# Two attention blocks on one core: octets of batches worked in turn by pairs, with K loaded for two octets at once

## The chip, the core and the metric

The kernel runs on one core of a Trainium2 chip. The core has a matrix engine (TensorE, PE in the profile), a vector engine (DVE), a scalar engine (ACT), a general engine (GpSimd, POOL) and a queue engine (SyncE, SP), which here issues all transfers between HBM and on-chip memory. PE writes its results to eight banks of accumulation memory (PSUM); DVE and ACT read them there. The metric is the device time of one execution in microseconds (us); lower is better.

## The reference

Two independent problems, A and B, of the same shape are computed and their outputs set side by side. One of them, cut to what matters:

```python
B, Sq, D = 16, 80, 576
Hq, Hkv, Sk, Dh = 32, 16, 512, 128           # two query heads share one K/V head
q = (x @ wq).reshape(B, Sq, Hq, Dh).transpose(0, 2, 1, 3)
k, v = repeat(k_cache, 2, axis=1), repeat(v_cache, 2, axis=1)
scores = einsum("bhqd,bhkd->bhqk", q, k) * Dh ** -0.5
o = einsum("bhqk,bhkd->bhqd", softmax(scores), v)
out = o.transpose(0, 2, 1, 3).reshape(B, Sq, Hq * Dh) @ wo
```

All tensors are bfloat16. K and V are 33.5 MB each for one problem, 134 MB together for both.

## The kernel before

**Units and octets.** The work is cut into 128 units. A unit is one batch row with four K/V heads, which is eight query heads. Eight units with the same four K/V heads and the batches of one half (0 to 7 or 8 to 15) form an octet; there are 16 octets. `unit(g)` (L372) orders them: problem, pair of head groups, half, head group within the pair. So octets 2i and 2i+1 have the same batches and neighbouring head groups; their K heads lie next to each other in HBM.

**Steps of a unit.** The 640 query rows of a unit (8 heads of 80) are held as five blocks of 128 rows, four from one K/V head each and a fifth with the 32 rows left over from each. K comes through a transposing transfer (`em_ldk`, L628, 512 KB) into one of NK = 7 slots of `kT`; V comes plainly (`em_ldv`, L632, 512 KB) into one of NV = 5 slots of `v_sb`. PE multiplies queries and K (L675 for whole blocks, L662 for the left-over block, two units at a time); DVE takes the row maximum (L684); ACT takes the exponential with a row sum (L688); DVE inverts the sums (L694); POOL scales the block (L697). PE transposes the five blocks (40 matmuls, L729), DVE or ACT moves the result to `pT` (L740 to L749), PE multiplies with V (16 matmuls, L772) and DVE or ACT moves that to `oT` (L786).

**Projections.** Queries for two batches and four query heads are one session of 16 matmuls (L544) and a tail of 4 (L559), moved to `qT` by ACT or DVE (L572, L573). Sessions run one per unit, about 11 units ahead of use (LQ = 11). The weights of one head group (`wq_sb`, 1 MB and two small `wt` pieces) have two slots and serve both halves. The output projection of a pair of head groups is 40 groups of 8 matmuls (L821, two per 128-row block and column half), whose results are kept (L832) or added and stored (L849, L855). Its weights come in four transfers (L600).

**What sets the order.** Every operation is put in a list with a stream name and a key (`S.add`). `arrange` (L176) then places all operations by the string ORDER: each letter takes the next operation of one stream, an apostrophe moves an operation from DVE to ACT (or to the other engine of its pair), and a digit names the PSUM bank. Each engine, SP among them, runs its operations in exactly that order, and `finalize` (L198) derives the waits. SP is one queue: while its next transfer waits for a slot, all transfers behind it wait too.

**Order of the units.** `steps` (L477) runs the first 12 octets one after another, all eight units of an octet before the next. The last four octets (two pairs, units 96 to 127) already go in turn: one unit of the first octet, one of the second, and so on. `sess` (L480) orders the query sessions to match.

Of the kernel before, what the change touches and what calls it, by code (L numbers as in the profile page):

```python
# [13 lines left out]
LA = 11.5  # L14
NK = 7
NV = 5
# [3 lines left out]
NS = 32  # L20
VK = 8.0
# [30 lines left out]
WQ1 = -16.8  # L52
# [8 lines left out]
nEJni7HHHHJHMak3j4LEMk4j5j7LKj5Hd3Jd6IdIj2'ABj1ad0Le6e5od3Llodd2'AK'Bd6lf0adpe4'Ad3omd5EBle2CdLuf0'Boe7'Ad4uoG  # L61
le1j3aole6d5CLle2uodd3'Bvple1d5NoumdAe7'Ad6old3BlCodug0245'Buld1xz'ye2Jk3d7Khwe5oadd3Alod4'ACBf06ludpd7upe1me2
d5o'Be0'Aoj4ldoc3'AcaCd1mCBuj7sle5vLd6Lludog2347'Bue0'wc6'xoulchd3tNhle2vCAd5a'youg16'zve0y'wd4u'Axld7o'Bf13zl
dpe2'Bc6pk5me0cCc7o'Aucmd1Ctuaj4loc7ucK'se3Ld2'suole7vg45olCe0u'zxe6hwd3C'Boauld5oue2'yAdlc7uoe1e4'Avoj0'BclLd
3olf05Ctuc6lpchd7ulsae1pmg26ome4ye0'w'xoc5'Ae2lod3'zod1lBe6cClouhg47atlvCe0ye5'w'xc2locd4'Bslc6CAvf12o'ze3ucpl
e0c7uCpcmc5uatc'sod1'tume7oug56loud2C'xz'yud3'wBlhue6e1holug05alw'ACCof67u'A'ye4pve2lovmoc1uc'xlCc6pue0c'zsd4u
loc5ute1mhcBe2uad6log37o'slCe0uwd5'xzluc1Coc'Be2u'ye7Ae6'td3ovlog14ulhoFd0lyFc2'xcF'zCBe1ud7lFswuc3ao'Ace2v'tf
56olg34Cplue1z'xumd2oc4cwlCe5Auo'yd0upc3ld1vB'scg57e4'yo'td5'ze3'wd7lAxe2o'Bb4Coluhbluhamg23Cue0b6ouqlbCuc4vqc
e0'sc6uocc4'yzc'te2h'sd3olac4xclwg06A'B'tf12w'ye5p'zd4xb6mpome0e1aob'Aloe2lCc7Bue5oclb3usloe0e1hCCc7loubaovlcq
ule2d5ou'tf06qlug17pme2zb3'wo'yae0'Ac7olce1bC'spulxoue2mc7e0ovd4lhCocvI'qe6d1lthuCBg37hluoaf25'ywuze0'x'Ab3upl  # L70
o'Bd4Cple1ud6Comuc7ce0luCc2cmubtoug25'qsulac7vye1e3oe0vb2oloblCule1qd3ho'zcad2xlCwe0vsc5'Aocug17'tC'Buf45'yzuc
6lpcuc7wcmpe0b1at'A'xo'se7md3o'Be6c4lblCve0h'qcc7Gusd5houchog24'tIulaf17y'w'zd6AlCe2e4uob3'xuBlpe0d5oc2coblsmp
g24lqe1wmc3Cocvd0'Aylue7d6xo'te1'ze2CBe3lb4oColavg57olue1wbzu'Ayuc7'qcole0ue2e5ohld4uhxd3ClBauc1o'scuog06lte7l
wc2Cocuc1'x'sAe5uc'zBd2lof46t'yd3Clpug17pmuhc5a'ywve0xe4CmAcud1o'Bue2slc3ocve6'zd5olg07Ctloe4d3'xz'yhe2'BChoc0
vlcIc7wouclac5e6tulcof47u'sAe2lc0pud1'spmcg56Comutd4luxe0d7'zo'yg26walCBue5A'xc1'yCue0woe3'zcvc2o'sd6luBcoc1'A
ue7hlcoac4d5lte0'scolg23Ctluf17wz'xue4'Ab0'yp'Bome2c3aoe6ld5Coue1lcpd4ule2obvmolg67h'qhle1xGb0wo'zI'yCae2Aud7'
BCole6ue5Coc4lcve1tbluovsc4lcCoc3u'scqe2lud4ouf06tlg15upue2'wb3'zAmb'yCovhe0e1aluob7ould5xp'Bd2lqc4e0mcog13'sC
Clve6e4'zobau'wouc3'qxcylue0d7Bluc1oc'Ad6'the2'sf45alg13pob0'zx'wCmBue3pbluCoc4ue2yld6vhoe1'Acaumqd3oc7lcg05ls
Cu'tf27z'ye1'xpd4Cb5omvpluae0bomuwe1Bu'Ac2ole7cc3o'qe6le0tchd5olag12lb7'sxo'Bze6lbCoue0lqd3uwc7o'ye2he6'ACocvl
ad5oulg14Cu'tf02wlzud7'Apu'xc4e6'Bpcme5b3oolhe0bCaolv'suc6qle5d4yumcg13tof02'ywxc6'zAe1'Bcohc7le4acColue3b5o't  # L80
ulsc7e1plcd4omc6Ccsvd3tupg07aCuCe6y'xb'wulzu'Bd0Come1ve7qld3oue2a'Ac5oulg46oulcCyb1v'wlxCuA'zf47Bushc6e0phue2c
hoe5mubJoluod3ltd4'qCpe0ulg26oud5'yze1mxe2wc6olcc7Acloe0c3'scold1Be6lCg24oua'tC'suCf07xlyue3'zpe2c6v'Boe4md1uo
'wclud0AJolvhg35thlupJe2c6'yxad4wmze3o'Be5c'Aoe0lc7cColuc2Cd1'svC'toclue7g36olud5uyle0Fsv'zd3xhwe2'BuoFc7'Ak6F
ouclg14FCKluhe0a'tuCe2'woc7'Avcz'yf56ulxd1ou'sc4plce0td7mpe2'Bog45mCoulc3cxe6zulc0co'Bd5'wyld7te2'sd4og36Ale0'
ze1ob2'wCylubCoue0aluc3ocb6'AuxlsvCBc5crue0e1obvohlue2hrd3lDCoe0uag67'toluf15x'zwd2'ype7lBd6omc3cAc0lsce1'tg34
ople0b7hwzDe1oac4bylCCc'xumre0d3ou'Bc7'Asd5ulocve2Clc4Coe1ue6a'tcolb0vo'sulg27uf14y'zub'wp'xuaAme2pc7clBd3rmd5
oe0g16lohle4Dzb2h'wx'yCDCoud6'tIBe0ulaf17ov'Ae5pblupme4Cd3ovmc1cule0sc7ucog15'turloe7b2a'x'yolze1e4lboole0e7rc
5'wCcB'Auhd2lohc3uohcle1Id4slCDog06uD'tCuaf57z'x'wud3Bpb6uCpmue4bo'AumCyvc5ld2vclc7ug01ruscc4'tze6ae5'x'wb7ool
e1bo'ylCBe0vcole2he6ud5oDlud1arlog07Alc2Csucc3'wz'tuf46xe2pb7Bmpbaome1rc'ye4Coe6lvc7d0o'Aucloe2ud5ClGtusDg17lo
huhe4'yzc3aclCe1oue7b6olvsc2uxf34o'Blcbtlpd5mrd7wAg26pCe0'xuc3'yBe1cmoud7'wc2lAcd4o'zaCg05sluCte6u'ywc3oe1'Avc  # L90
'xe0ole2uc7olhd6zhle1BacCd5ov't'soluf07e4lupg23oumpc1'x'ycBd0lwze2c5'scCmoe4uc3e1Ah'tue7lCacod5u'sColg26uoluc3
zcle4uwe1od6'Av'xd7y'Ble0og25h'tolDc4cI'ye3sc1ald2Cwvo'xe4'ze0Aucld5ou'tCof36luc1plcuc4Bc'sCe0amCug17o'tvple3b
# [174 lines left out]
def bass_concat_heads__gqa_block_cached__gqa_block_cached__near_ridge_kernel(  # L267
# [27 lines left out]
    with ExitStack() as es:  # L295
# [32 lines left out]
        def R(res, ver):  # L328
            return (res, ver)
# [151 lines left out]
        for g_ in range(NG - 2 * NPP):  # L481
            for m_ in range(8):
                sess[g_, m_] = g_ * 8 - LQ + m_
# [450 lines left out]
```

## Time and profile before

| | us |
|---|---|
| median of 3 runs | 745.14 |
| lowest and highest of them | 742.85, 745.35 |
| the profiled execution | 743.02 |
| its span, first to last instruction | 741.1 |

The profile page gives, for that execution, the busy time of each engine and groups of instructions by source line with their count and mean duration. Matmuls are pipelined: the mean of one (233 ns for a matmul of 160 columns) is its whole passage, and the next one starts well before it ends. The chain of waits lists instead what each step added to the chain that ended last, which for a row of matmuls is their pace. A view by windows gives busy time, granted PE clock (1.00 in the whole run) and transfer rate in stretches of the span.

### The profile page before, as it was taken

The page shows a single profiled execution, that of the slowest core. Times are in us where ns is not written, and L with a number is a line of the kernel's source. Part 1 is how long each engine was busy: PE and PEld are TensorE (multiplying, and loading weights), DVE is VectorE, ACT ScalarE, POOL GpSimd, SP SyncE. Part 2 cuts the span into 40 slices and gives each one's busy share as a digit, 9 for nine tenths or more (in the row PEclk, how much of TensorE's full clock was granted, in tenths as well). Part 3 has the DMA queues.
Part 4 walks back from the last instruction along what each step waited for, and adds up shares of the span by engine and source line. Part 5 has one row for each costly group of instructions (what it writes and reads, how often), then busy time and mean ns, then how long its engine had stood idle before and what let it go on. Part 6 is the DMA issues. An engine that isn't in the chain of part 4 may idle for free.

```text
span 741.1 us, 28948 instructions
## 1 busy us (share of the span) xinstructions
PE 728.4 (98%) x12103; PEld 565.7 (76%) x12103; DVE 643.0 (87%) x1469; ACT 640.6 (86%) x1835; POOL 433.8 (59%) x650
## 2 busy tenths in 40 slices
PE   7999999999999999999999999999999999999998
PEld 5777677787777777777787767777878777778777
DVE  2999788899789989899888998889988798899994
ACT  2999788899888988789878998799988898899994
POOL 0557537566556745646665564565754664657783
PEclk9999999999999999999999999999999999999999
DMA  8999999989998959999968999999999799999970
GB/s 222 225 225 237 262 234 256 227 172 264 217 201 210 265 127 209 243 263 219 232 142 202 234 298 216 224 257 240 209 215 224 155 227 236 201 216 207 238 211 22
DMA packets 364402, 160.91 MB, mean 217 GB/s; under 512 B 276464, under 2 KB 360688, under 8 KB 364272
## 3 DMA queue, kind: packets, MB, share of 16 engines
q1 hardware_dynamic: 364272, 159.05, 99.2%
q8 instruction: 96, 1.57, 0.9%
q14 instruction: 34, 0.28, 0.1%
HBM read 87.65 MB, written 2.95 MB: 122 GB/s over the span
## 4 chain that ended last, share of the span: by engine, by line
PE 84%; ACT 11%; DVE 3%; DMA 1%; issue 0%; SPq 0%; POOL 0%
PE ps L821 19%; PE ps L544 18%; PE ps L772 16%; PE ps L675 13%; PE ps L729 9%; ACT p_sb L688 7%; PE ps L559 4%; PE ps L662 4%; ACT pT L740 2%; DVE negmax L684 2%; ACT oT L786 1%; DMA acc<-in_A_x_dram 1%; ACT qT L572 1%; DVE pT L742 1%; DVE qT L573 0%
## 5 line engine op out<-in xcount | busy, mean ns | idle before, releaser
L697 POOL TENSOR_SCALAR p_sb<-p_sb,rinv 128x512 bf16<-128x512 bf16 x640 | 432.0, 695 | 289.4 <-DVE rinv L694 288.9
L688 ACT ACTIVATE p_sb<-ps,negmax 128x512 bf16<-128x512 f32 x640 | 444.2, 712 | 48.0 <-DVE negmax L684 43.8
L684 DVE TENSOR_REDUCE negmax<-ps 128x1 f32<-128x512 f32 x640 | 420.5, 682 | 36.5 <-PE ps L675 24.9
L772 PE MATMUL ps<-pT,v_sb 128*128 128x160 bf16 x2048 | 193.1, 233 | 1.6 <-issue 0.8
L544 PE MATMUL ps<-xT,wq_sb 128*128 128x160 bf16 x2048 | 180.4, 234 | 1.3 <-ACT pT L740 0.4
L821 PE MATMUL ps<-wo_sb,oT 128*128 128x288 bf16 x1280 | 180.9, 286 | 0.0
L675 PE MATMUL ps<-kT,qT 128*128 128x512 bf16 x512 | 179.6, 381 | 0.6 <-ACT p_sb L688 0.2
L772 PEld LDWEIGHTS ps<-pT,v_sb 128*128 128x128 bf16 x2048 | 152.5, 98 | 33.8 <-ACT p_sb L688 3.0
L544 PEld LDWEIGHTS ps<-xT,wq_sb 128*128 128x128 bf16 x2048 | 149.0, 98 | 26.4 <-ACT pT L740 2.0
L821 PEld LDWEIGHTS ps<-wo_sb,oT 128*128 128x128 bf16 x1280 | 122.0, 98 | 41.5 <-ACT oT L786 1.1
L688 ACT ACTIVATION_READ_ACCUMULATOR p_sb<-ps,negmax 128x1 f32 x640 | 144.1, 225 | 0.0
L740 ACT COPY pT<-ps 128x512 f32<-128x512 f32 x152 | 89.7, 607 | 11.2 <-PE ps L729 10.5
L729 PE MATMUL ps<-ident,p_sb 64*128 64x64 bf16 x5120 | 96.1, 190 | 0.3
L729 PEld LDWEIGHTS ps<-ident,p_sb 64*128 64x128 bf16 x5120 | 88.2, 95 | 2.8 <-issue 0.8
L742 DVE COPY pT<-ps 128x1024 bf16<-128x1024 bf16 x104 | 70.6, 684 | 12.5 <-PE ps L729 10.0
L572 ACT ACTIVATE qT<-ps 128x320 bf16<-128x320 f32 x135 | 59.5, 455 | 12.9 <-PE ps L559 11.5
L786 DVE CAST oT<-ps 128x320 bf16<-128x320 f32 x123 | 58.9, 481 | 9.2 <-PE ps L772 8.7
L675 PEld LDWEIGHTS ps<-kT,qT 128*128 128x128 bf16 x512 | 48.3, 97 | 22.2 <-ACT p_sb L688 3.9
L786 ACT CAST oT<-ps 128x320 bf16<-128x320 f32 x133 | 57.7, 445 | 8.4 <-PE ps L772 7.7
L573 DVE TENSOR_SCALAR qT<-ps 128x320 bf16<-128x320 f32 x121 | 57.7, 481 | 6.7 <-PE ps L559 3.6
L749 DVE COPY pT<-ps 128x256 bf16<-128x256 bf16 x138 | 37.7, 283 | 10.6 <-PE ps L729 9.4
L694 DVE RECIPROCAL rinv<-rowsum 128x3 f32<-128x3 f32 (+1 forms) x256 | 38.5, 160 | 4.0 <-ACT p_sb L688 3.8
(33 smaller groups left out, 199.1 us busy)
## 6 DMA issues: line engine op xcount, KB each, us to landing
v_sb<-in_A_v_cache_dram SPq DMA_DIRECT2D x64, 512.0 KB, 4.9
v_sb<-in_B_v_cache_dram SPq DMA_DIRECT2D x64, 512.0 KB, 4.9
wo_sb<-in_A_wo_dram SPq DMA_DIRECT2D x8, 576.0 KB, 7.5
wo_sb<-in_B_wo_dram SPq DMA_DIRECT2D x8, 576.0 KB, 6.8
wq_sb<-in_B_wq_dram SPq DMA_DIRECT2D x4, 1024.0 KB, 7.0
wq_sb<-in_A_wq_dram SPq DMA_DIRECT2D x3, 1024.0 KB, 8.3
out_dram<-osb SPq DMA_DIRECT2D x40, 72.0 KB, 4.0
wq_sb<-in_A_wq_dram SPq DMA_DIRECT2D x4, 256.0 KB, 3.2
```

The source lines that it names most:

```text
L544: last = e.matmul(ps[:, vbq[h].phys, QO + 160 * r:QO + 160 * r + 160], lhsT=wq_sb[:, wsl, ck, hi * 128:(hi + 1) * 128], rhs=xT[:, half, ck ...
L572: return e.activation(dst, src, AF.Identity, scale=SCALE)
L675: return e.matmul(ps[:, vb.phys, :], lhsT=qT[:, qsl, bl, gl * 160:gl * 160 + 128], rhs=kT[:, ks, :, gl * 128:(gl + 1) * 128], start=True, ...
L684: return e.tensor_reduce(negmax[:, si:si + 1], ps[:, vb.phys, :], axis=AX.X, op=AluOpType.max, negate=True)
L688: return e.activation(p_sb[:, psl, :], ps[:, vb.phys, :], AF.Exp, bias=negmax[:, si:si + 1], scale=1.0, accum_out=rowsum[:, ss, k:k + 1])
L697: return e.tensor_scalar(p_sb[:, psl, :], p_sb[:, psl, :], rinv[:, ss, k:k + 1], 1.0, op0=AluOpType.mult, op1=AluOpType.mult)
L729: last = e.matmul(dst, lhsT=p_sb[64 * h:64 * h + 64, psls[k_], j * 128:(j + 1) * 128], rhs=ident[64 * h:64 * h + 64, 64 * h:64 * h + 64], ...
L740: return e.copy(pT[:, pts, :, :].bitcast(F32)[:, :, 32 * h:32 * h + 32], ps[:, vtp[h].phys, :].rearrange("p (n c) -> p n c", n=16))
L742: return e.tensor_copy(pT[:, pts, :, 64 * h:64 * h + 64], psb[:, vtp[h].phys, :].rearrange("p (n c) -> p n c", n=16))
L772: last = e.matmul(ps[:, vo.phys, off:off + 160], lhsT=v_sb[:, vs, gl, j * 128:(j + 1) * 128], rhs=pT[:, pts, 4 * gl + j, :], start=(j == 0 ...
L786: return (e.copy if en == "act" else e.tensor_copy)(dst, src)
L821: last = e.matmul(ps[:, vb.phys, 0:DC], lhsT=oT[:, hi, rb * 128:(rb + 1) * 128], rhs=wo_sb[:, wi, c3 * DC:(c3 + 1) * DC], start=(hi == 0), ...
```

## The change

All 16 octets go in turn by pairs (ILV = 0), not the last four alone. One transposing transfer of 1 MB brings the K heads of both octets of a pair for one batch, so there are 64 K transfers for 128 units. `kT` holds three such buffers (NK = 6 units, where there were 7), and V has six slots (NV = 6, where there were 5). A unit reads its K half from the shared buffer through `k_of`: rows of 128 keys lie 1,024 elements apart there, where they lay 512 apart. A buffer is refilled when both units have read it. The weights of the second head group are loaded earlier (WQ1), since the second octet now starts with the first. ORDER is written anew, as are the engines and the banks that it names.

```diff
-NK = 7
-NV = 5
+NK = 6
+NV = 6
+ILV = 0
-WQ1 = -16.8
+WQ1 = -21
 ORDER = """
...
-        kT = sb("kT", [128, NK, 4, 512], BF16)
+        kT = sb("kT", [128, NK // 2, 4096], BF16)
...
-        steps = [(g_, b_) for g_ in range(NG - 2 * NPP) for b_ in range(8)]
-        for g_ in range(NG - 2 * NPP, NG, 2):
+        steps = [(g_, b_) for g_ in range(ILV) for b_ in range(8)]
+        for g_ in range(ILV, NG, 2):
             steps += [(g_ + i_ % 2, i_ // 2) for i_ in range(16)]
...
+        def k_of(U, g4):
+            pr_, r_ = divmod(U % NK, 2)
+            if steps[U][0] >= ILV:
+                return kT[:, pr_, :].rearrange("p (j n) -> p j n", j=4)[:, :, r_ * 512 + g4 * 128:r_ * 512 + g4 * 128 + 128]
+            return kT[:, pr_, r_ * 2048:(r_ + 1) * 2048].rearrange("p (j n) -> p j n", j=4)[:, :, g4 * 128:(g4 + 1) * 128]
...
-            def em_ldk(e, kc_ap=kc_ap, b=b, q=q, ks=ks):
-                src = kc_ap[b, 4 * q:4 * q + 4, :, :].rearrange("g (p j) d -> (g p) j d", j=4)
-                return e.dma_start_transpose(kT[:, ks, :, :], src)
+            def em_ldk(e, kc_ap=kc_ap, b=b, q=q, ks=ks, w=2 if goct >= ILV else 1):
+                src = kc_ap[b, 4 * q:4 * q + 4 * w, :, :].rearrange("g (p j) d -> (g p) j d", j=4)
+                dst = kT[:, ks // 2, ks % 2 * 2048:(ks % 2 + w) * 2048].rearrange("p (j n) -> p j n", j=4)
+                return e.dma_start_transpose(dst, src)
...
-            S.add("sp", 5.0 * gfirst[U] + 0.5 * (U - gfirst[U]) - LA - KK, em_ldk, writes=[R(("kT", ks), U)],
-                  dsem="d_k%d" % ks, name="ldk%d" % U, stream="K")
+            if goct < ILV or U % 2 == 0:
+                S.add("sp", 5.0 * gfirst[U] + 0.5 * (U - gfirst[U]) - LA - KK, em_ldk,
+                      writes=[R(("kT", (U + i_) % NK), U + i_) for i_ in range(2 if goct >= ILV else 1)],
+                      dsem="d_k%d" % ks, name="ldk%d" % U, stream="K")
...
-                                                    rhs=kT[:, ks_, :, g4 * 128:(g4 + 1) * 128],
+                                                    rhs=k_of(U_, g4),
...
-                                        rhs=kT[:, ks, :, gl * 128:(gl + 1) * 128], start=True, stop=True)
+                                        rhs=k_of(U, gl), start=True, stop=True)
```

The order in which SP issues its first transfers, before (left) and after (right), by the names of the code; a number is the unit, the octet or the half:

```
x half 0, first part               x half 0, first part
wq octet 0, piece 0, two wt        wq octet 1 (1 MB)
wq octet 0, piece 1                x half 0, second part
x half 0, second part              wt octet 1, wq octet 0 piece 0, wt octet 1, two wt octet 0
wq octet 0, piece 2                wq octet 0, pieces 1 to 3
K 0                                K 0 and 1 (1 MB)
wq octet 0, piece 3                x half 1, first part
x half 1, first part, two wt       K 2 and 3
K 1, K 2                           x half 1, second part
wq octet 1 (1 MB)                  V 0, V 1
K 3, x half 1 second part          K 4 and 5
V 0, K 4, K 5                      V 2, K 6 and 7
V 1, V 2, K 6, K 7                 V 3, two wo, K 8 and 9
```

More of the change, by code (lines that the diff above doesn't have):

```diff
@@ L66 @@
[L66 to L80, printed above, removed]
@@ L126 @@
[L126 to L128 removed]
+nEJni7GJIHIHMHj3k4Hj5LLHEHad3j7Md5j6k2LKdd4A'Bj6d3Ldj5A'Bd6d3dd4Bd1dd3A'B'AJKd0LaEdd4'A'Bd5e0e1odf2'Aod3lpe7d4
+lodme0Ad6'Boe1ld3BJloe2hdhCe7old4uaoe0lvd5Cole1NudAf2ld7up'Be6ouj0md3Llodf02'ABd1'Bp'Ak3j4lpd5CmLdue7Be6md4ou'
+Ae0CCd5loudKvlhAg1237oaN'Be4u'wj6x'zk5oe1ule2j7LuK'yolg0356LlCof47u'xz'yc1uclpj3vd5CLme2upc6e3'w'suoe4cmd1holF
@@ new lines @@
+g07CouFltc2av'ycxe6B'wd3u'zse0loc7d2olce1ltg46o'Ae0le7od5'zc1Colucc6scluxd0Ct'wv'yf17A'Budpe6'Be2ud3Cpme0uoc4m
+cud1A'sholg57FCoFlue4zad6'yvolf27uwc5lpcd0A'x'tpe4mg35o'Bd2C'zyve1lwc5uocme3c4suc'Aoe5ld7te6loe4b1xo'Ble3Cobul
+oub5lqhCluhe0e1hoe6ug34aolbCo'xu'yClue0qd3w'Bvd5'zAoulf17g24ulppmc6cc0scc1'tzc'xe6'sd0Cwumoc4e1u'ycod7'Avltc2e
+3Bclhog46hCsalue1wc5o'xe2u'ycd3z'Bv'Ae4tle7d6Coub5oluoe0lbolc4'qcf12'slg57pCe4uy'xb0'wmBhuC'zhod5uhc7Alcavpe1e
+6boutle4Coe3ud7mquc1olcg02vo'slCc6uyce1x'te4uzd0'wlod6'Be2olb3olc7Cue1lbou'Ach'qf25shlg34apCpc7u'zcb1C'wC'yuA'
@@ new lines @@
+xmve0e4od3muc2t'Bucold5vslf67ug02pub'wz'xmpc4'Be2q'ye6oe5h'Acd1holhd3Colug02lud6y'tv'we5'zxc4Bcmc2oe0e3'sCcoau
+c7'tcAle4ue2oc1lcsd5olg07tob3'x'zy'wlBe1e0oblCoulc7he2e5uhocc4v'se1qclCd7uth'Ad3Coluf06olug24Cplub5'zumve1e4'x
+oab'yu'wCpluc2comud0sc1'qe6le2ocd5'Atlg47o'BCf16uw'ze3lpub7'yCAvmoe2e0ve4ob'xluoc1uC'qcle3usd7aolc1ucp'Bd2log0
+5tld4z'xe1'wB'yd3Cmoe0uc5oclug26slAIf15C'zxGue7'ye0hob6v'BIoluhe2Ce3plbuo'wumd7CAv'qe0oc4lcuoc6lcutc2clpe1e4oa
+d3's'tog06ld2'wz'yd1xmBc6e0lAe3cCoue7'sg45Colvoc6'zuce0'ytd5uloe6ub4hlCoIule3e7uob'xa'wlvBCd0'AqulCf16ovg24plu
@@ new lines @@
+c3'yzuce7mwd2xuCo'sc4'Bce1'td3olg04AhlGe7'yc5Ccx'zvpb1wumoe0e4uobluole6uc7o'qcld0tc1A'Bf47'slcpe2'sd3Comug56pl
+ue1xc4'zwaco'ye2d6t'Aloc5cc4lsce0Bd5mCove1g23tluof47u'zwAe0lb3pI'xo'Bhe1mbhCou'yhpe6hluc4oe2cld5Covle0d1saulqg
+46ouCe2'wxub3'yBmuoe1lc4oblzclc7e0d6'qo'Ace1'sc3oe2lcd5t'tlog07f34w'zxe1'Ab7'yolCCe0ublouplc6ve1cmoad2uCd0Clqu
+sc3'Bcug67'tuf15'zxupe3'yb7u'w'BAmvoc6ce0C'sd4uhole2hvbolhuhpld3qg06Cpuc7'wzu'xd2'yAc'Be0mhe6oc3c'td4ole1sc7lC
+coug03htluCe6yd7'wv'x'zAe1d0umoc3uocle2Bc5'scole6hg34Ctlauof15'wvC'Axb2zlup'Bue7e6'yobumolc3qce0ld4oe1e2Csld6v
@@ new lines @@
+og37upub0xmBole6e5abzlo'wc7'yCcqu'Ae1oc3le0ud4old6ole2c'tc5sclCg17ou'thf03v'ywhAe5'xu'ze1ob4lCo'Bc7lcCpvd6se2m
+uc5ocld7uhte0lug15oauCle2wbuo'zuyle0d5Ad1xCC'Boue2'qg67pulob4u'w'yzlue0bomCAle2uFc7ocFve6'sd3oFluf07FCqlve5pc4
+'xcupd6'tmBc2cog14'slc2ye0'x'zcwe5oe1'Ad4moc3clCBd7vtlc6ouJe0e2'scoulg35tulof16'wC'zyd0u'ACe5xlue3Bc4cpud7h'sC
+oe2umJb4Joulaoe1ulbolpg35lre2w'ze4Cyc1u'xb5ovAbluComue0rcld3uoe2'Bvd5loag46le0z'tc7'xe2'ywcoc6'se1k4olcd7o'Ac0
+lBcCd3Kluf25'tvhCsg14DupDc6wuhcz'Ad0mupd4'xCymug27Buf15t'x'Bc3p'ye6caoc4mcsd2'twle1e4b3'zCo'Aue7oe0lvboluod6lr
@@ new lines @@
+g14lphe7z'yc3Dc'wohme0c4hb1olCAlue5xcoe2u'te7ad0'sCBule4obuolvc3Colce2urc6lcoue1e7sd5log34'tColuf26C'zvb1'x'wu
+'yAe4lpue0d3oDubholvc7'Brcle4d5oamg01slb7y'z'wp'Ae0c4Come1ucbltuoe2d3loe0d4rDlohe1'xg67hCBluhof25'wDu'zAc0'yCc
+pue7'sc3Cd6lxvoc'Buc0mthcd4Cuplg13u'suc7z'x'we0'ycvoe2'Be3ac1'Auoe4lcoc6lctd0Cmse7vd2olug15Ctluf36z'w'xu'yb4o'
+AuBle0e1hod5hc7plce2Csbmvouod7lurg03lpDe1'ze4oc2'yce3x'thb0o'walAe2Blc5obolcCre1luc7oe4d3uold2Csclue0Cg15'toum
+uf47'w'yb6vpGxumCDe1pbhvlAIoue4'zId3Blue0Cod5uCrg12luoDb6'xau'Blue5bmo'ze0c7'yod4lre1colc2e6cCslud5Co'tg07u'wl
@@ L129 @@
+e2suc7locDug0136ho'tluhf47xyDlc1e5we3p'zcc2o'se0e6mcoc1hlcCtc4ucolvt'splug2345ome1b0Cwluoe2'zyue7e6lbo'xolg134
+5rloDc2e0'yxacCwe7lvof34'zCuCc1ob6lvplue0pcme5Cubomuoe7lc3tue4rclc1usDco'shug0256'tolue1b3zlo'we7'ye0xCboluolu
+e2rg1456lCoDuf37'xh'zCwc0uCp'ye1cule6oe5b4vmpovlc2csublouClg0136rvDe4'ywc5uthc'zoe0uc3'scxmCug1256tlouc7c'ywe3
+zuc4'xlcsg1256o'tc7C'xy'zcue0'sc4wovclc7tculc6sb5Cubucg2347tb0y'z'x'wc7cc3scbtrb7DrDbb5brDrD
 """
@@ L475, in bass_concat_heads__gqa_block_cached__gqa_block_cached__near_ridge_kernel @@
                   name="xte%d" % half, stream="xe2")
-        steps = [(g_, b_) for g_ in range(NG - 2 * NPP) for b_ in range(8)]
-        for g_ in range(NG - 2 * NPP, NG, 2):
+        steps = [(g_, b_) for g_ in range(ILV) for b_ in range(8)]
+        for g_ in range(ILV, NG, 2):
             steps += [(g_ + i_ % 2, i_ // 2) for i_ in range(16)]
         sess = {}
-        for g_ in range(NG - 2 * NPP):
+        for g_ in range(ILV):
             for m_ in range(8):
                 sess[g_, m_] = g_ * 8 - LQ + m_
-        for g_ in range(NG - 2 * NPP, NG, 2):
+        for g_ in range(ILV, NG, 2):
             for i_ in range(16):
@@ L659, in em_qkr @@
                             last = None
-                            for _, vb_, ks_, qsl_, bl_, _ in group:
+                            for U_, vb_, ks_, qsl_, bl_, _ in group:
                                 for g4 in range(4):
```

90 lines of the change are left out of this document (36 added, 54 removed).

## The prediction

> **What bounds the kernel now.** I read the page's busy times first, then the chain of waits, PE's groups by line in two stretches of the span, and last the transfers. The page says that PE is nearly always occupied, with DVE and ACT not far behind:
>
> ```profile
> PE 728.4 (98%) x12103; PEld 565.7 (76%) x12103; DVE 643.0 (87%) x1469; ACT 640.6 (86%) x1835; POOL 433.8 (59%) x650
> DMA packets 364402, 160.91 MB, mean 217 GB/s; under 512 B 276464, under 2 KB 360688, under 8 KB 364272
> q1 hardware_dynamic: 364272, 159.05, 99.2%
> ```
>
> PE's 98% hides gaps, because a matmul's record spans its whole passage. The chain of waits shows the pace of each kind of matmul where nothing holds it up (start, us, what):
>
> ```profile
> 29.85 0.55 PE ps L662 x8
> 31.30 0.43 PE ps L675 x2
> 297.93 0.24 PE ps L559 x4
> 479.99 0.98 PE ps L821 x8
> 481.40 1.11 PE ps L544 x16
> 482.75 0.58 PE ps L729 x40
> 489.79 0.55 PE ps L772 x8
> ```
>
> So a matmul of L544 or L772 costs 0.069 us, L821 0.1225, L675 0.215, L662 0.069, L559 0.06, L729 0.0145. A unit has 16 of L544, 16 of L772, 10 of L821, 4 of L675, 4 each of L662 and L559 and 40 of L729: 1.11 + 1.11 + 1.225 + 0.86 + 0.275 + 0.24 + 0.58 = 5.40 us. 128 units are 691 us of PE work, which the change leaves as it is. The span is 741.1 us, so about 50 us are start, tail and gaps; only these can be won.
>
> Where the gaps are is seen by counting PE's work in two stretches. The first runs from the first transposition of unit 8 to that of unit 96 (72.3 to 572.1 us; 3520 transpositions are 88 units, or 11 octets), where octets go one after another:
>
> ```profile
> L772 PE MATMUL ps<-pT,v_sb 128*128 128x160 bf16 x1416 | 134.9, 233 | 0.8 <-issue 0.8
> L821 PE MATMUL ps<-wo_sb,oT 128*128 128x288 bf16 x896 | 126.9, 286 | 0.0
> L544 PE MATMUL ps<-xT,wq_sb 128*128 128x160 bf16 x1408 | 123.7, 233 | 1.1 <-ACT pT L740 0.4 <-DVE qT L573 0.3 <-issue 0.3
> L675 PE MATMUL ps<-kT,qT 128*128 128x512 bf16 x351 | 123.4, 381 | 0.6 <-ACT p_sb L688 0.2
> L729 PE MATMUL ps<-ident,p_sb 64*128 64x64 bf16 x3520 | 66.1, 190 | 0.1
> L559 PE MATMUL ps<-xT,wt 64*128 64x160 bf16 x356 | 27.8, 234 | 1.0 <-ACT qT L572 0.4 <-ACT oT L786 0.2 <-POOL p_sb L697 0.2
> L662 PE MATMUL ps<-kT,qT 128*32 128x512 bf16 x352 | 27.1, 384 | 0.6 <-ACT p_sb L688 0.3 <-ACT oT L786 0.2
> ```
>
> By the prices above this is 98.3 + 109.8 + 97.7 + 75.5 + 51.0 + 21.4 + 24.3 = 478 us of work (0.5 more for ten small transposes) in 499.8 us: 21.3 us of gaps, 1.94 us per octet. The second stretch, 572.1 to 664.7 us, holds units 96 to 111, which the kernel before already works in turn:
>
> ```profile
> L821 PE MATMUL ps<-wo_sb,oT 128*128 128x288 bf16 x192 | 27.5, 286 | 0.0
> L772 PE MATMUL ps<-pT,v_sb 128*128 128x160 bf16 x256 | 24.3, 233 | 0.0
> L675 PE MATMUL ps<-kT,qT 128*128 128x512 bf16 x64 | 22.4, 380 | 0.0
> L544 PE MATMUL ps<-xT,wq_sb 128*128 128x160 bf16 x256 | 22.3, 233 | 0.0
> L729 PE MATMUL ps<-ident,p_sb 64*128 64x64 bf16 x640 | 11.9, 190 | 0.0
> L662 PE MATMUL ps<-kT,qT 128*32 128x512 bf16 x72 | 5.5, 384 | 0.0
> L559 PE MATMUL ps<-xT,wt 64*128 64x160 bf16 x68 | 5.3, 234 | 0.0
> ```
>
> That is 23.5 + 17.8 + 13.8 + 17.8 + 9.3 + 5.0 + 4.1 = 91.2 us of work in 92.6: 0.7 us of gaps per octet. So the trace of before holds a sample of the changed order, and its PE is fuller. The longest waits of ACT and DVE, and two stretches of equal length (length, then busy PE, weight loads, DVE, ACT, POOL, then clock, DMA share, GB/s), say what the gaps hang on:
>
> ```profile
> ACT p_sb L688 <- DVE negmax L684: 43.8, 73, 1.8
> DVE negmax L684 <- PE ps L675: 24.9, 52, 2.0
> 253.00:344.10 91.10, 90.08 (x1512) 69.86 (x1510) 83.36 (x188) 77.38 (x223) 52.78 (x79) 1.00 0.97 210
> 572.10:664.70 92.60, 92.60 (x1548) 73.39 (x1546) 80.76 (x181) 81.10 (x234) 54.88 (x82) 1.00 1.01 212
> ```
>
> Score blocks queue at DVE (ACT waits for the maximum 73 times), a PSUM bank comes free late, and PE misses it. DVE is 91.5% busy in the first of these stretches and 87.2% in the other, while ACT goes the other way. No row shows PE waiting for a K or V transfer after the start.
>
> **The change, part by part.**
>
> *In turn, and the new order.* Eleven octets, those from unit 8 to unit 95, change from one kind of order to the other. If each comes down from 1.94 to 0.7 us of gaps, 13.4 us go; if the new order is no smoother than the old, nothing. Below nothing is excluded only by DVE's and ACT's unchanged number of maxima and exponentials (640 each), so I let a loss of 2 us stand. The built order speaks for the gain: priced by the mean durations of their groups, DVE's and ACT's work exceeds PE's within stretches of two units by 15 us in all, where it did by 27. I take 1.13 us, two thirds of the way, since the sample is 16 units alone: 11 x 0.81 = 8.9 us won. What is late next is DVE again.
>
> *K in 64 transfers of 1 MB, three buffers.* The bytes are the same, and the pieces too: K comes in rows of 256 B before and after. SP's own time:
>
> ```profile
> 4.95 3.61 SPq L630 DMA_TRANSPOSE kT<-in_A_k_cache_dram  x1
> 302.43 6.13 SPq L630 DMA_TRANSPOSE kT<-in_A_k_cache_dram  x2
> SPq L630 <- PE ps L772: 39.9, 12, 4.0
> DMA to landing us min/median/max: 4.3/6.5/12.5
> ```
>
> Two K issues in a row hold SP for 6.13 us, 3.1 each, so one of 1 MB should hold it about 6 us, and V, wq and stores behind it wait that long. V has six slots now; in the built order there are 26 us of PE work (median) between the moment SP can reach a V transfer and its use. For K that window shrinks. A buffer is free when both units have read it; from there (or from what SP must wait for ahead of it) to the first matmul that needs the new K lie 15.6 us of PE work in the median, where it was 23.5, or 16.7 us of time at 741/691. A 1 MB transfer needs about 6.1 + (6.5 - 3.1) = 9.5 us from issue to landing. The narrowest window, 9.8 us of work or 10.5 us, just holds it; five of 61 are under 12.4 us. The ends: 0 us lost if 9.5 holds; if landing takes the longest seen plus the second half, 12.5 + 3.1 = 15.6 us, 19 windows are too short by 34 us in all, of which I count half, since a stall also lengthens the next window: 17 us. The price is nearest to the row of two back-to-back issues; I take 0.5 us for a queue that is now and then fuller.
>
> The Trainium skill says in "DMA: Bandwidth & Descriptors", section "Rules for kernel authors", that most bandwidth needs 128 partitions and at least 1 MiB per DMA. The rows above do not bear on 1 MB transposes; since pieces stay at 256 B, I give the rule no part in the sum. By the figure of 261 GB/s for transposes in its section "Latency and other measured facts", 1.05 MB would take an estimated 4.0 us to move, and the 0.5 us would be 0.
>
> *The start.* The second octet now starts with the first, and SP brings its weights first.
>
> ```profile
> L675 PE MATMUL ps<-kT,qT x512: 379/379/391, 14.6 to 726.3; 128*128 128x512 bf16 x171
> 0.00:20.00 20.00, 15.76 (x128) 10.27 (x128) 6.28 (x18) 5.78 (x14) 1.69 (x9) 1.00 0.90 230
> 20.00:50.00 30.00, 29.91 (x499) 23.16 (x496) 27.51 (x64) 27.69 (x80) 19.09 (x30) 1.00 1.13 214
> 50.00:100.00 50.00, 47.41 (x860) 35.55 (x858) 41.69 (x96) 44.55 (x130) 28.40 (x42) 1.00 1.13 248
> ```
>
> Ahead of the end of the first K there are 4.14 MB in SP's queue (2.18 before); at 230 GB/s that is 18.0 us, so the first score matmul starts at 18 to 19 us, not 14.6. PE is not idle for it: 12 half sessions and 5 tails stand ahead of that matmul, where 3 and 1 did, which is 9 x 0.55 + 4 x 0.24 = 5.9 us of work pulled forward. PE would gain about 2 us here. Next, K for units 8 and 9 stands after 12.35 MB: 20 x 0.230 + 30 x 0.214 = 11.0 MB at 50 us, and 1.33 / 0.248 = 5.4 us more, 55.4 us. The PE work ahead of its first use is about 43 us, so PE cannot be less than 12 us behind its work there, about where the kernel before is. DVE and ACT get their first block 3.4 us later, and this may carry through the first 60 us. Ends: 2 us won, 3.4 us lost, and I take 1 us lost.
>
> *The tail.* Between the transposition of unit 112 and that of unit 120 the new order gives DVE 87 operations, where it was 82, 39 of them maxima (37 before) and 7 wide copies (3):
>
> ```profile
> L684 DVE TENSOR_REDUCE negmax<-ps 128x1 f32<-128x512 f32 x640 | 420.5, 682 | 36.5 <-PE ps L675 24.9
> ```
>
> At 0.68 us for a maximum, and about the same for a wide copy, less three projections and moves, that is 2.9 us more DVE work in a stretch that has little PE work to hide it. Ends 0 and 2.9; I take 1.5.
>
> *Sum.* -8.9 + 0.5 + 1.0 + 1.5 = -5.9 us against the profiled execution's 743.0 us: **737 us**. That execution lies 2.1 us under the median of 745.1, as the lowest run does; from the median it would be 739. I keep 737.
>
> **The rivals.**
>
> *R1, the gaps stay.* The smaller gaps of the last octets would come from what stands in them and not from working in turn. For it: a single stretch of 16 units is the evidence. Against it: DVE's share in the table. Then 743.0 + 0.5 + 1.0 + 1.5 = 746 us.
>
> *R2, slower: K comes too late.* Three buffers give a window of 16.7 us in the median, and a 1 MB transfer behind V transfers may take 15.6 us. It decides from about 12.4 us on; at 15.6 it costs 17 us, 737 + 17 = 754 us. For it: landings of up to 12.5 us for half the bytes, and a DMA share of 1.13 in whole stretches of the start. Against it: 9.5 us from the rows of a free queue, and mean DMA shares near 1.0 later. The Trainium skill speaks for this side in "Perfetto Trace Analysis", section "DMA Optimizations": splitting transfers lets some work start sooner; here they are merged.
>
> *R3, the full gain.* All eleven octets reach 0.7 us of gaps and start and tail cost nothing: 743.0 - 13.4 = 730 us. For it: the built order's overloads of DVE and ACT are nearly halved. Against it: the added K limit.
>
> **How the numbers follow.** The forecast gets 0.50, R1 0.20, R2 0.18, R3 0.12. The forecast's own range is 732 to 742: its terms add from -13.4 to its small losses, without R2's price. The range for 8 in 10 runs from 729, under R3, to 752, which leaves out the worse part of R2. A change of 0.5% (3.7 us) is about what a measurement of this kernel can tell from none. Faster by more than that (under 741.4) are R3 and 0.46 of the forecast: 0.58. Within it lie 0.04 of the forecast and 0.11 of R1: 0.15. Slower (over 748.9) are R2 and 0.09 of R1: 0.27.
>
> **What would show it.** Right: PE's work counted as above between units 8 and 96 leaves about 12 us of gaps, not 21; ACT's wait for the maximum is well under 43.8 us; K issues take about 6 us each and land within 10; the first score matmul starts at 18 to 19 us. Wrong: PE, or its weight loads, waiting for K transfers at the score matmuls anywhere after the first 60 us, which would be R2; or fewer waits of ACT for DVE and yet the same gaps, which would leave the PSUM banks as a cause unproved.

## The result and the profile after

The changed kernel takes 734.64 us (median of 4 runs, 733.71 to 736.21), the kernel before, run beside it, 744.82 us (742.85 to 745.35). The ratio is 0.987, with a 95% interval of 0.9845 to 0.9896: faster by 10 us, where 6 to 8 were forecast (737 us against the profiled 743.0 or the median of 745.1). The profiled span fell from 741.1 to 732.0 us.

PE's groups of the changed kernel between the first transposition of unit 8 and that of unit 96 (74.0 to 564.5 us; columns as in the prediction's fences; line numbers have moved by 6 to 9, so L781 is the old L772):

```profile
L781 PE MATMUL ps<-pT,v_sb 128*128 128x160 bf16 x1416 | 131.6, 233 | 0.1
L830 PE MATMUL ps<-wo_sb,oT 128*128 128x288 bf16 x896 | 127.7, 286 | 0.0
L684 PE MATMUL ps<-kT,qT 128*128 128x512 bf16 x355 | 122.4, 380 | 0.0
L550 PE MATMUL ps<-xT,wq_sb 128*128 128x160 bf16 x1408 | 122.3, 233 | 0.0
L738 PE MATMUL ps<-ident,p_sb 64*128 64x64 bf16 x3522 | 66.3, 190 | 0.7 <-issue 0.7
L565 PE MATMUL ps<-xT,wt 64*128 64x160 bf16 x356 | 27.8, 234 | 0.0
L671 PE MATMUL ps<-kT,qT 128*32 128x512 bf16 x352 | 27.1, 384 | 0.0
```

By the prediction's prices this is 479.4 us of work (ten small transposes among it) in 490.5 us. The gaps are 11.1 us, 1.01 per octet, where they were 21.3 and 1.94. The same count says where the span's 9.1 us come from: 10.2 here, 1.6 at the start, less 1.0 between units 96 and 112 and 1.7 in the tail.

The page of the changed kernel (engines, the transfer queue, the chain that ended last), and then four lines of its waits (total us, times, longest):

```profile
PE 719.2 (98%) x12103; PEld 565.2 (77%) x12103; DVE 639.3 (87%) x1457; ACT 646.7 (88%) x1847; POOL 433.9 (59%) x650
q1 hardware_dynamic: 362224, 159.05, 92.7%
PE 94%; DMA 2%; ACT 1%; DVE 1%; issue 1%; SPq 0%
```

```profile
DVE negmax L693 <- PE ps L684: 27.1, 61, 2.9
ACT p_sb L697 <- DVE negmax L693: 21.4, 50, 2.0
PE ps L671 <- DMA kT<-in_A_k_cache_dram: 1.7, 1, 1.7
PE ps L550 <- DMA wq_sb<-in_A_wq_dram: 1.6, 1, 1.6
```

ACT waits half as long for the maximum (43.8 before), and PE waits for K once, ahead of unit 8. Next, SP's K issues with their landing, the first score matmul, and three windows of the start:

```profile
L637 SPq DMA_TRANSPOSE kT<-in_A_k_cache_dram x32: 3885/5616/8895, 8.0 to 337.4; - x32
L637 SPq DMA_TRANSPOSE kT<-in_B_k_cache_dram x32: 3992/5008/6577, 347.5 to 697.2; - x32
...
DMA to landing us min/median/max: 6.0/8.1/12.3
```

```profile
L684 PE MATMUL ps<-kT,qT x512: 376/379/391, 17.8 to 717.5; 128*128 128x512 bf16 x171
```

```profile
0.00:20.00 20.00, 16.20 (x176) 11.24 (x177) 6.34 (x17) 5.00 (x11) 1.32 (x8) 1.00 1.05 256
20.00:50.00 30.00, 29.36 (x497) 21.77 (x496) 29.05 (x69) 29.74 (x87) 18.76 (x29) 1.00 1.16 237
50.00:100.00 50.00, 47.05 (x812) 36.93 (x805) 41.43 (x94) 41.97 (x123) 29.12 (x43) 1.00 1.11 265
```

The chain of waits has K for units 8 and 9 from 40.65 us to its landing at 53.0 (start, us, what):

```profile
40.65 12.35 DMA kT<-in_A_k_cache_dram
```

### The profile page after: what moved, and what is told of

It is laid out like the page before. It is cut to its first block, busy times and chain, and to the rows that moved or that the text cites. A ratio compares the mean times of both kernels' runs of the same rounds, so it can differ in the third digit from the quotient of the medians.

```text
span 732.0 us, 28848 instructions
## 1 busy us (share of the span) xinstructions
PE 719.2 (98%) x12103; PEld 565.2 (77%) x12103; DVE 639.3 (87%) x1457; ACT 646.7 (88%) x1847; POOL 433.9 (59%) x650
## 3 DMA queue, kind: packets, MB, share of 16 engines
q1 hardware_dynamic: 362224, 159.05, 92.7%
## 4 chain that ended last, share of the span: by engine, by line
PE 94%; DMA 2%; ACT 1%; DVE 1%; issue 1%; SPq 0%
PE ps L830 22%; PE ps L781 19%; PE ps L550 18%; PE ps L684 15%; PE ps L738 10%; PE ps L671 5%; PE ps L565 4%; DMA kT<-in_A_k_cache_dram 2%; DMA wt<-in_A_wq_dram 1%; ACT p_sb L697 1%; DVE negmax L693 0%; ACT qT L578 0%; DVE oT L795 0%; SPq L514 0%; ACT pT L749 0%
## 5 line engine op out<-in xcount | busy, mean ns | idle before, releaser
L781 PE MATMUL ps<-pT,v_sb 128*128 128x160 bf16 x2048 | 191.0, 233 | 2.2 <-ACT pT L756 1.2
L830 PE MATMUL ps<-wo_sb,oT 128*128 128x288 bf16 x1280 | 181.4, 286 | 0.0
L550 PE MATMUL ps<-xT,wq_sb 128*128 128x160 bf16 x2048 | 178.2, 233 | 1.7 <-DMA wq_sb<-in_A_wq_dram 1.6
L781 PEld LDWEIGHTS ps<-pT,v_sb 128*128 128x128 bf16 x2048 | 152.7, 98 | 34.2 <-issue 3.5
L684 PE MATMUL ps<-kT,qT 128*128 128x512 bf16 x512 | 177.2, 380 | 0.0
L830 PEld LDWEIGHTS ps<-wo_sb,oT 128*128 128x128 bf16 x1280 | 121.1, 98 | 44.4 <-ACT pT L756 2.5
L697 ACT ACTIVATION_READ_ACCUMULATOR p_sb<-ps,negmax 128x1 f32 x640 | 140.9, 220 | 0.0
L749 ACT COPY pT<-ps 128x512 f32<-128x512 f32 x165 | 96.5, 601 | 10.5 <-PE ps L738 9.8
L578 ACT ACTIVATE qT<-ps 128x320 bf16<-128x320 f32 x140 | 62.0, 453 | 17.8 <-PE ps L565 14.2
L795 DVE CAST oT<-ps 128x320 bf16<-128x320 f32 x132 | 63.5, 481 | 9.5 <-PE ps L781 8.4
L751 DVE COPY pT<-ps 128x1024 bf16<-128x1024 bf16 x91 | 62.1, 682 | 9.9 <-PE ps L738 8.7
L795 ACT CAST oT<-ps 128x320 bf16<-128x320 f32 x124 | 53.9, 442 | 10.4 <-PE ps L781 9.5
L579 DVE TENSOR_SCALAR qT<-ps 128x320 bf16<-128x320 f32 x116 | 55.3, 481 | 6.0 <-PE ps L565 2.6
L671 PE MATMUL ps<-kT,qT 128*32 128x512 bf16 x512 | 40.0, 384 | 2.2 <-DMA kT<-in_A_k_cache_dram 1.7
```

Source lines behind the costliest of these rows:

```text
L550: last = e.matmul(ps[:, vbq[h].phys, QO + 160 * r:QO + 160 * r + 160], lhsT=wq_sb[:, wsl, ck, hi * 128:(hi + 1) * 128], rhs=xT[:, half, ck ...
L671: last = e.matmul(ps[32 * g4:32 * g4 + 32, vb_.phys, :], lhsT=qT[:, qsl_, bl_, g4 * 160 + 128:g4 * 160 + 160], rhs=k_of(U_, g4), start=Tru ...
L684: return e.matmul(ps[:, vb.phys, :], lhsT=qT[:, qsl, bl, gl * 160:gl * 160 + 128], rhs=k_of(U, gl), start=True, stop=True)
L697: return e.activation(p_sb[:, psl, :], ps[:, vb.phys, :], AF.Exp, bias=negmax[:, si:si + 1], scale=1.0, accum_out=rowsum[:, ss, k:k + 1])
L749: return e.copy(pT[:, pts, :, :].bitcast(F32)[:, :, 32 * h:32 * h + 32], ps[:, vtp[h].phys, :].rearrange("p (n c) -> p n c", n=16))
L751: return e.tensor_copy(pT[:, pts, :, 64 * h:64 * h + 64], psb[:, vtp[h].phys, :].rearrange("p (n c) -> p n c", n=16))
```

## The experiments

Not all of a gap is a wait. In both traces the passage between a full matmul and one that uses part of the array (L662, L559, L729) costs about 0.10 us: from L544 to L559 it is 0.165 us from start to start, from L544 to L544 0.069. The prices of the three lines hold part of this already. Units 8 to 96 have 235 such passages before and 222 after (those between L662 and the other two counted in, those from L559 to L729, which cost nothing, left out). What exceeds the usual (median) interval of its pair of matmuls by over 15 ns I call a stall. Counted from the traces, stalls of units 8 to 96, in us and number:

```
before                    10.2 us in 59     after                       1.7 us in  12
  half the maximum         9.1 us in 49       K in halves               3.9 us in  15
  half the exponential     8.0 us in 35       no later K                2.4 us in  10
  both                     6.3 us in 22       no later K, few proj.    32.9 us in 102
  no later K               8.4 us in 52
```

So 8.5 of the 10.2 us are stalls, and 13 fewer passages are 1.3 more. What the stalled matmuls waited for can be found, since the kernel's order gives the bank of each group of matmuls. Laid over the trace before, 49 stalls of 7.6 us in all are at matmuls that start within 0.25 us, mostly 0.06 us, after the last read of their bank ended (0.48 us is the median of the others). ACT was the last to read in 6.2 of these 7.6 us, DVE in the rest. Of the changed kernel's stalls 0.3 us are of this kind. What went is mostly waits of PE for PSUM banks.

**Does the merged transfer bring the gain?**

```diff
-            def em_ldk(e, kc_ap=kc_ap, b=b, q=q, ks=ks, w=2 if goct >= ILV else 1):
+            def em_ldk(e, kc_ap=kc_ap, b=b, q=q, ks=ks, w=1):
...
-                dst = kT[:, ks // 2, ks % 2 * 2048:(ks % 2 + w) * 2048].rearrange("p (j n) -> p j n", j=4)
+                dst = kT[:, ks // 2, :].rearrange("p (j n) -> p j n", j=4)[:, :, ks % 2 * 512:ks % 2 * 512 + 512]
...
-            if goct < ILV or U % 2 == 0:
+            if True:
...
-                      writes=[R(("kT", (U + i_) % NK), U + i_) for i_ in range(2 if goct >= ILV else 1)],
+                      writes=[R(("kT", (U + i_) % NK), U + i_) for i_ in range(1)],
```

(and each "a" of ORDER doubled)

> The changed kernel with its order, but each 1 MB K transfer is issued as two of 512 KB in a row, one per unit, into the same three buffers. Theory T (the gain comes from working in turn and from the new order, the merged transfer only has to be in time): 734 to 738 us, gaps between units 8 and 96 still near 11 us. Rival M (the gain comes from the merged transfer, which uses the DMA engines better): most of the 10 us goes, 742 to 746 us, and PE waits for K at score matmuls in many places. For K itself: each half takes SP about 3.5 us, as in the kernel before, and the second half lands 7 to 9 us after the first one's issue.

Measured: 735.80 us, ratio to before 0.9866 (0.9841 to 0.9891), the same as with the merged transfer. SP's rows of this run:

```profile
L637 SPq DMA_TRANSPOSE kT<-in_A_k_cache_dram x64: 1763/3268/6952, 7.9 to 347.9; - x64
L637 SPq DMA_TRANSPOSE kT<-in_B_k_cache_dram x64: 1866/3102/8107, 352.4 to 701.4; - x64
...
DMA to landing us min/median/max: 4.4/6.1/11.4
```

The gain is not the transfer's. Two halves hold SP for 6.2 to 6.5 us, one of 1 MB for 5.0 to 5.6.

**What does K cost?** In both kernels the K transfers after the first buffers were left out.

```diff
-            if goct < ILV or U % 2 == 0:
+            if U < NK and U % 2 == 0:
```

(in the kernel before `if U < NK:`; in both, the letters of these transfers go from ORDER, and the score matmuls wait for the first K of their slot only)

> The changed kernel without the K transfers from the fourth on (29 of 32 MB of K left out; later units score against the first K in the buffers, so the output is not the reference's). PE's, DVE's and ACT's work is unchanged. Theory T (K costs PE only the wait ahead of units 8 and 9 and little else): 1 to 3 us off, 731.5 to 733.5 us. Rival R2 in a weak form (K is late in many windows and keeps part of the gain): 725 to 730 us.

> The kernel before without its K transfers from the eighth on (121 of 128 units' K left out; output not the reference's). The changed kernel won 5.4 us by the same edit. Theory C (what K costs is about the same in both, most of it at the start, so K is not where the 10 us come from): 739 to 741.5 us. Rival D (the kernel before loses its time to K transfers that are late or crowd the DMA engines, and the change's fewer, earlier ones end that): 729 to 735 us, near the changed kernel without K.

Measured: 729.25 us for the changed kernel, 5.4 less, which lies in the range that I had given to the rival; 741.75 us for the kernel before, 3.6 less than the 745.38 beside it. The rival's reason does not hold: the stalls of units 8 to 96 did not fall (1.7 and 2.4 us, of which 2.0 are one pause at 150 us that the trace gives as PE's own issue); those ahead of unit 8 fell by about 3, those behind unit 96 by about 2. That trace is of the slowest of four runs (731.21), so where the rest of the 5.4 us lies is not seen. Without K the two kernels are 12.5 us apart, so rival D falls: by these medians K costs the changed kernel 1.8 us more than it cost before. The 1.5 of the forecast's K and start terms is near this, but the start term itself came out the other way (below).

**Is it DVE's lateness?**

```diff
-    return e.tensor_reduce(negmax[:, si:si + 1], ps[:, vb.phys, :], axis=AX.X,
+    return e.tensor_reduce(negmax[:, si:si + 1], ps[:, vb.phys, 0:256], axis=AX.X,
```

> The kernel before with the row maximum taken over 256 of the 512 scores of a row (the softmax stays a softmax, since any shift cancels; DVE reads half as much). A maximum should fall from 0.68 us to about 0.4, 640 of them or about 180 us less of DVE. Theory T (the 1.94 us of gaps per octet come from score blocks that wait for DVE and give their banks back late): the gaps between units 8 and 96 come down from 21 to 12 us or less, 731 to 736 us. Rival S (the gaps come from the order in which PE meets its operands, whatever DVE's speed): 741 to 744 us.

> The changed kernel with the same cheaper maximum. Theory T (the change has taken away most of what DVE's lateness costs): it gains clearly less than the kernel before does by the same edit, 1 to 5 us, 730 to 734 us, and the two kernels come closer together than 10 us. Rival S: nothing, 734 to 735 us, and the difference to the kernel before stays at 10 us.

Measured: 742.89 us against 745.93 beside it, ratio 0.9957 (0.9938 to 0.9976): 3.0 us won. Changed kernel: 732.42, 2.2 won, not clear of the noise (731.1 to 734.1 against 733.7 to 736.2). A maximum fell to 0.417 us, as its group in the kernel before with the edit shows:

```profile
L684 DVE TENSOR_REDUCE negmax<-ps 128x1 f32<-128x256 f32 x640 | 256.6, 417 | 105.0 <-PE ps L675 82.1
```

164 us less of DVE's busy time (420.5 before) won 3. DVE's speed alone is not what the gaps hang on; theory T falls here.

**ACT alone, and both.**

```diff
-    return e.activation(p_sb[:, psl, :], ps[:, vb.phys, :], AF.Exp, ...
+    return e.activation(p_sb[:, psl, 0:w], ps[:, vb.phys, 0:w], AF.Exp, ...    # w = 512 if U < 4 else 256
```

> The kernel before with the exponential taken over 256 of a row's 512 scores from the fifth unit on (the other half of the probabilities is left over from earlier units, so the output is not the reference's). An exponential takes ACT 0.71 us; it should fall to about 0.5 us, some 130 us less of ACT. DVE's maximum is unchanged. Theory A (after a maximum of 0.42 us won only 3 us: the banks come back late because ACT is late with the exponentials and evictions): gaps between units 8 and 96 from 21 to 13 us or less, 732 to 737 us. Rival O (neither engine's speed counts; the gaps lie in PE's own order, or in transfers): 741 to 744 us.

> The changed kernel with the same shorter exponential. Theory A: it gains little, 0 to 3 us, 731 to 734.5 us, since working in turn has already taken the queue off ACT; the difference to the kernel before with the same edit shrinks to 5 us or less. Rival O: also little, but the difference to the kernel before stays near 10 us.

> The kernel before with both edits at once: row maximum and (from the fifth unit on) exponential over 256 of 512 scores; half of the probabilities is left over, so the output is not the reference's. Alone they won 3.0 and 5.3 us, and PE's stalls between units 8 and 96 stayed at the same matmuls, nearly all of them in stretches where no output projection (L821) is in PE's order. Theory P (in these stretches DVE and ACT both have more work than PE, so each alone keeps PE waiting): together they win at least their sum, 8 us or more, 733 to 737 us, and the stalls go. Rival O (they are waits fixed by the order, whoever is fast): no more than the better one alone, 739 to 742 us.

Measured: before with the shorter exponential 740.12 us against 745.38, 5.3 won; the changed kernel 733.12, 1.5 won, so the two are still 7.0 apart; before with both edits 738.00 against 745.06, ratio 0.9905 (0.9871 to 0.9939), 7.1 won. None reaches its theory's figure in full: DVE won 3.0, ACT 5.3, both 7.1, where the change itself wins 10. The intervals are wide (3.1 to 7.0 us for ACT, 4.5 to 9.6 for both), so that both win more than ACT alone is not shown, and 7.1 is no more than the sum of the two. With both, 6.3 of the 10.2 us of stalls stay, where theory P had them go. Each edit alone leaves most stalls at the same matmuls. Where they are shows in windows of the kernel before: first its engines (as in the prediction), then L821, the output projection, alone (busy time and count, clock, DMA share, GB/s):

```profile
243.00:264.00 21.00, 19.84 (x388) 14.64 (x388) 19.47 (x48) 20.32 (x58) 15.09 (x23) 1.00 1.10 275
264.00:294.00 30.00, 30.00 (x492) 23.70 (x493) 26.91 (x61) 24.31 (x70) 14.85 (x23) 1.00 0.71 147
422.00:455.00 33.00, 31.52 (x541) 23.66 (x539) 29.05 (x68) 29.68 (x86) 20.64 (x31) 1.00 1.15 257
```

```profile
243.00:264.00 21.00, 0.00 (x0) 1.00 1.10 275
264.00:294.00 30.00, 10.14 (x72) 1.00 0.71 147
422.00:455.00 33.00, 3.51 (x28) 1.00 1.15 257
```

PE has holes where it has few or no output projections (called projections from here on), and ACT is 90 to 97% busy there. Of the 10.2 us of stalls, 6.2 lie in the 12 of 44 pairs of units without a projection. The longest five intervals from one projection matmul to the next are 25.7 to 37.6 us in this stretch; in the changed kernel none is over 15.2. The same windows of L830 there:

```profile
243.00:264.00 21.00, 4.57 (x32) 1.00 0.94 232
264.00:294.00 30.00, 6.89 (x48) 1.00 1.03 236
422.00:455.00 33.00, 8.57 (x61) 1.00 0.99 234
```

One pause does not fit: units 22 to 25 of the kernel before have no projection and no stall.

The exponential's group in the kernel before with both edits, and its first window:

```profile
L688 ACT ACTIVATE p_sb<-ps,negmax 128x256 bf16<-128x256 f32 (+1 forms) x640 | 307.6, 489 | 79.2 <-DVE negmax L684 67.1 <-PE ps L729 9.2
```

```profile
243.00:264.00 21.00, 20.89 (x414) 17.14 (x415) 16.22 (x50) 17.26 (x63) 13.40 (x21) 1.00 1.03 273
```

With both faster the hole of 1.16 us is down to 0.11.

**Spreading the projections in the kernel before.** This needs PSUM banks chosen anew, so a control went with it: the same order, with new bank digits only, given by my model of which bank comes free first (one line of ORDER's 68):

```diff
-ze1ob2'wCylubCoue0aluc3ocb6'AuxlsvCBc5crue0e1obvohlue2hrd3lDCoe0uag67'toluf15x'zwd2'ype7lBd6omc3cAc0lsce1'tg34
+ze1ob2'wCylubCoue0aluc5ocb3'AuxlsvCBc6crue7e1obvohlue2hrd5lDCoe0uag37'toluf16x'zwd2'ype3lBd0omc5cAc4lsce1'tg37
```

> Control for the next run: the kernel before with its order unchanged, only the PSUM bank of each group of matmuls chosen anew by one rule (the bank that came free first). If banks alone were the matter, 735 to 740 us; by theory P, nothing: 743 to 747 us.

> The kernel before, octets one after another as before, banks by the same rule as the control; the output projections of the first six half batches are moved later so that they spread over the stretches that had none (the longest stretch without any falls from 7.7 to 5 units of attention work, most others from 5.5 to under 2; the last two half batches stay). Nothing else moves. Theory P (the gain of the change is that working in turn spreads the output projections): most of the stalls between units 8 and 96 go, 4 to 8 us under the control. Rival O (the gain comes from working in turn itself): within 2 us of the control.

Measured: the control 807.22 us, 62 more than before; the spread order 883.43. Both expectations failed. With the control spoilt, the second run says nothing about projections. Counted as above, 53.0 us of the control's stalls in units 8 to 96 are at matmuls whose bank has just been read out, where it was 7.6. The weight loads ahead of score matmuls show a part of it, in the control's waits and in those of the kernel before:

```profile
PEld ps L675 <- ACT p_sb L688: 20.7, 41, 1.0
```

```profile
PEld ps L675 <- ACT p_sb L688: 3.9, 10, 0.5
```

**Projections taken away instead.** In the changed kernel, with order and banks as they are, and no K to be late:

```diff
-                                for hi in range(sp_ * hs, (sp_ + 1) * hs):
+                                for hi in ((0, HH - 1)[sp_:sp_ + 1] if cut else range(sp_ * hs, (sp_ + 1) * hs)):
```

(cut is true for the first problem's second pair of head groups)

> The changed kernel without the later K transfers (as in the run of 729.25 us), and with 14 of every 16 matmuls of the output projections of the first problem's second half left out (280 matmuls of 0.1225 us, 34.3 us of PE work, over about 28 units from unit 40 on; evictions stay; the output is not the reference's). Order, banks and DVE's and ACT's work are those of the changed kernel, octets go in turn, no K is late. In the kernel before PE lost about 0.42 us per unit where it had no projections (2.5 us in units 68 to 73). Theory P (what decides is whether projections stand beside the attention work, since without them DVE and ACT have more work per unit than PE): PE stalls here too, some 0.4 us per unit, and only about 23 of the 34 us are won, 704 to 708 us. Rival O (working in turn itself keeps PE supplied, with or without projections): the whole 34 us, 694 to 698 us.

Measured: 726.11 us against the 729.25 of the run without later K: of 34.3 us of work taken away, 3.1 are won. Windows of the run without later K, and of this one:

```profile
250.00:300.00 50.00, 50.00 (x845) 39.27 (x845) 44.26 (x99) 46.73 (x134) 29.12 (x44) 1.00 0.37 115
```

```profile
250.00:300.00 50.00, 43.84 (x748) 30.36 (x740) 45.19 (x104) 46.97 (x137) 30.25 (x46) 1.00 0.42 130
```

DVE and ACT hardly go faster when PE is freed: the stalls grow by 30.5 us, and 28.6 us of stalls lie in the ten pairs of units that lost projections, nearly all at banks just read out. Rival O falls for this order: in turn as it is, its attention work alone does not keep PE supplied. Theory P had the right mechanism and a loss per unit that was too small (0.4 us; it is 30.5 / 28 = 1.1). Here the projections stand in time that DVE and ACT need anyway. Two limits: the order was built for the projections and one built without them was not tried; and the ten pairs of units that have none in the changed order as built stall for 0.4 us in all, with 7.9 maxima in a pair, where pairs beside 32 matmuls of the projection have 11.5. So a short pause is bridged.

**A try at a better start.** The "a" of K 8 and 9 was moved ahead of the first two wo transfers ("F") in ORDER.

```diff
-Ae0CCd5l...uoe4cmd1holF
-g07CouFltc2av'ycxe6B'w...
+Ae0CCd5l...uoe4cmd1hola
+Fg07CouFltc2v'ycxe6B'w...
```

> The changed kernel with the K transfer of units 8 and 9 moved ahead of the first two wo transfers in SP's order, nothing else. In the changed kernel's trace PE waits 1.9 us before the first score matmul of unit 8. Theory S (that wait is on the path): it goes, 732.5 to 734 us. Rival N (the time is taken back a few us later, because wo or the next K is late in its stead): 734 to 736 us.

Measured: 734.18 us, ratio 0.985 (0.9827 to 0.9873), not to be told from the changed kernel. The wait before unit 8 is gone from the trace, and stalls of 1.1, 1.4 and 2.0 us begin at 39, 46 and 70 us, where the changed kernel has 1.4 at 69. The time is taken back as rival N says, but its reason is not shown: the trace names PE's own issue and ACT there, and no transfer. (It is of the slowest of five runs, 737.29 us.) No run that does the whole computation is clearly faster than the changed kernel.

## Why the prediction was right

*In turn and the new order* (8.9 us forecast): 10.2 won, at 1.01 us of gaps per octet against 1.13. The size came from the sample of units 96 to 111, and the sample was good: those 16 units had no stall at all before, only passages. R3's full gain is not reached by 0.3 us per octet, and R1 falls. (R3's 13.4 us would be 11 x 1.24 = 13.6 by the printed figures.) The reason given was half right. Banks come free late and PE misses them, as it says: 7.6 us of such stalls before, 0.3 after. That DVE's queue is behind this, and that "what is late next is DVE again", failed: ACT read last in 6.2 of the 7.6 us, and a shorter maximum won 3.0 us where a shorter exponential won 5.3. The measure in the same step, DVE's and ACT's work together against PE's within two units, names both engines; that they limit jointly is argued, since both together won 7.1, no more than the sum. What the runs point to is the even mixture: projections, PE work that asks little of DVE and ACT, no longer pause for 26 to 38 us. Whether it is this spreading, working in turn as such, or the banks and engines that the new ORDER names was not separated; the run meant for it was lost to the banks.

*K* (0.5 us lost): issue took 5.0 to 5.6 us for the 6 forecast, landing 8.1 for 9.5, and PE waited for K once, 1.7 us. No row of either trace has PE waiting for V, with five slots or with six. R2 falls, and its price with it. The term itself was not measured apart from the start; the runs without K give 1.8 us for both. The Trainium skill asks in "DMA: Bandwidth & Descriptors", section "Rules for kernel authors", for at least 1 MiB per DMA where bandwidth is to be highest. The trace agrees in the transfers (the queue's packet time fell from 99.2% to 92.7%, and is 99.9% with halves; two halves hold SP longer than one whole) and not in the time: with halves it is 735.8 us.

*The start* (1.0 lost): 1.6 won. The first score matmul came at 17.8 us for the 18 worked out, but K 8 and 9 landed at 53.0 and not at 55.4, since the queue moved 256 and 237 GB/s in the first 50 us and not 230 and 214. The rate, taken from the kernel before, was the term that was mis-sized. The size of the K transfers is not the reason: with K in halves the new order moves 236 and 244 GB/s there. Why it moves more stays open.

*The tail* (1.5 lost): 1.7. *Units 96 to 111* (no term): 1.0 lost, most of it in one stall at 591 us, which stands in the trace as PE's own issue.

*The sum.* The profiled spans differ by 9.1 us, where the sum had 5.9. Of the 3.2 us more, 2.6 are the start, which was forecast with the wrong sign, and 1.3 the first term; the others take 0.7 back. The first term came out near its size although its reason named DVE alone: it was read off the sample, whatever the reason, and that is in part luck. The range of 732 to 742 us held, but it was a choice: the ends of the terms, with K at 0.5, add to 728 and 752.

## What to carry to other kernels

Where PE is 98% busy and two other engines are near 90%, ask which work of PE the others don't need, and whether it is spread evenly: the mean shares hide pauses in it, and a window of that line alone shows them. Halving one engine's work tests that engine alone, and here said less than a look at the stalled matmuls: how long before each start its bank was read out, and by which engine. Test a queue by taking the transfers out, not by their busy share.

## What the runs showed that I had not expected

- Bank numbers alone cost 62 us. In the kernel before a PSUM bank is taken again 0.48 us (median) after it was read out, and banks are held more than 80% of the time, both counted from the trace. That my model was wrong by some tenths of a us per bank is the likely reason, and was not tested.
- Taking 280 matmuls away from a PE that is 98% busy won 9% of their time.
- One transposing transfer of 1 MB lands in 8.1 us (median), one of 512 KB in 6.1 to 6.5: the second half costs 2 us, not the 3.1 that I took.
- In two runs (K 8 and 9 moved, and the changed kernel with the shorter exponential) PE stands still for 2.0 us for nothing that the profile shows, at the matmul of the stall at 591 us; what it waits for stays open. PE's waits of the first of them:

```profile
PE ps L671 <- issue: 2.0, 1, 2.0
```
